# A retention and SoLU kernel: 17 activation tiles transposed by DMA, 16 variances on ScalarE, three more load buffers

## The chip, the cores and the metric

The kernel runs on one core of a Trainium2 chip. The metric is the device time of one execution in microseconds (us), lower is better. A core has TensorE (PE in the profile, with its weight loads as PEld), VectorE (DVE), ScalarE (ACT), GpSimd (POOL), SyncE (SP, which here issues nearly all DMAs) and 16 DMA engines. SBUF is the on-chip memory, PSUM the memory that TensorE writes.

## The reference

Eight batches of eight heads, 576 positions, head size 64; then a feed-forward layer over the 4608 tokens, 512 wide with 1024 inner units.

```python
scores = scale * np.matmul(q, k.transpose(0, 1, 3, 2))
Dmat = np.where(rel >= 0, gamma[:, None, None] ** rel[None, :, :], 0.0)
x = np.matmul(scores * Dmat, v)            # then heads side by side: 4608 x 512
h = x @ w_in
e = np.exp(h - h_max)
solu = h * (e / (np.sum(e, axis=-1, keepdims=True) + 1e-09))
mu, var = mean(solu), mean((solu - mu) ** 2)
out = ((solu - mu) / np.sqrt(var + 1e-06) * g_ln) @ w_out
```

## The kernel before, in words

The sequence of a batch is cut into windows of 256 positions; the last 64 positions of four batches are put together to one more window. That makes 18 windows, and with the two halves of the heads 36 **steps** i. A window has 256 tokens, two **tiles** t of 128 tokens, 36 tiles in all. Tile t belongs to window t//2, so it needs the attention of the steps 2(t//2) and 2(t//2)+1.

Per step: loads of q, k and v by SP (`load`, L373; a step of the joint windows takes four DMAs each) into pool raw, five buffers for each of the three; casts with decay factors on POOL (sq, sk in `scale` L389, cv in `cast_v` L397); transposes T of q and k on PE (`qk_tp` L413), evicted by ACT into pool ev (`tl_ev` L451); scores S on PE (`scores` L499) into the one buffer of PSUM pool s; the mask on DVE (`mask` L536); I, the part that comes from the state (`inter` L475), V, the masked scores times v (`av` L514), and K, the new state (`kv_mm` L524), into pool xy; st, sm, sc on DVE and POOL for the state; xe, the eviction of the attention to xT on ACT (`x_ev` L573).

Per tile: M1 on PE (`mm1` L581, eight matmuls of 512 columns) into the one buffer of pool h; ex on ACT (`exp_` L592); so on DVE (`solu` L597), an f16 tile of 128 x 1024 in pool solu, four buffers; the variance, either bnA and bnB on DVE (`stats` L612) or, for the tiles listed in VA (0 to 3), va on ACT (`squares` L620) with the row sum from so's accumulator and a small fin on DVE (`final` L635); fx on ACT and rs on POOL (`rstd` L644) give the scale of the row, once for a pair of tiles; L, the transposes of solu on PE (`ln_tp` L434), 32 small ones of 64 x 64; Le, its eviction; M2 on PE (`mm2` L653, eight matmuls) with oe on ACT (`o_ev` L664) and the store out (`store` L673), osb having three buffers. M2 writes a buffer of pool s, that of S too; from tile 31 on, odd tiles use pool xy.

From step 10 on, T of step i and L of tile i-6 share one PSUM tile (pool tl, one buffer), and one ACT instruction, TL, evicts both into one buffer of ev. The tiles 30 to 35 have a Le of their own. L of tile t stands ahead of T of step t+6, and M2 of tile t four M1 later than M1 of tile t.

The order on each engine comes from `plan` (L122) and `order_ops` (L233): lists FIRST and LAST fix it by hand for the beginning (on PE to M1 of tile 14) and the end; between them every operation has a due time, and `order_ops` sets the order by the costs of the table DUR. PE's order in the middle is M1, M2, I, L, T, V, K, S (where a tile or step of that kind is there). Six stores (tiles 22 to 27) go as two DMAs of 64 rows (L678). Filling matmuls with zeros (L844) keep PE busy early.

Of the kernel before, what the change touches and what calls it, by code (L numbers as in the profile page):

```python
# [13 lines left out]
P = 128  # L14
# [3 lines left out]
for _b in range(0, B, 4):  # L18
# [5 lines left out]
    T=0.26, L=0.26, Tw=0.45, Lw=0.45, I=0.22, V=0.23, K=0.13, S=0.22, M1=1.73, M2=1.73, M2h=0.87, oeh=0.42, G=0.1, WM=1.73,  # L24
    TL=1.03, Te=0.58, Le=0.58, xe=0.74, ex=1.22, oe=0.69, va=1.25, wiA=0.62, wiB=0.45, wg=0.68, wgD=0.43,
    cvA=0.62, mask=1.22, st=0.58, so=1.22, soA=1.3, bnA=0.68, bnB=0.89, fx=0.2, fin=0.42, wc=0.74, wm=0.62,
    sqD=0.75, gc=0.17, cvD=0.45, sq=1.04, sk=1.04, cv=0.61, sm=0.42, sc=0.81, rs=0.69, rsB=1.0,
    ldx=0.88, ldw=1.36, out=0.65,
)
HOP, PE_OUT = 0.07, 0.2  # L30
# [3 lines left out]
VA = (0, 1, 2, 3)  # L34
ON = {'sq0': 'DVE', 'sq1': 'DVE', 'cv0': 'ACT', 'cv1': 'ACT', 'sk2': 'DVE', 'sk3': 'DVE', 'cv2': 'ACT', 'cv3': 'ACT', 'cv4': 'ACT', 'cv5': 'ACT', 'cv6': 'ACT', 'cv7': 'ACT'}
CAP = dict(
    rawq=5, rawk=5, rawv=5, q16=3, k16=4, v16=4, ev=8, s=1, ret=2, xy=1, gg=6, gt=2, s160=4, s161=9, h=1,
    e=2, solu=4, osb=3, tl=1, tlx=2, tlT=1, tlL=1, wst=5,
# [3 lines left out]
FIRST = dict(  # L42
    PE=(
# [5 lines left out]
    ),  # L49
    ACT=(  # L50
# [4 lines left out]
    ),  # L55
    DVE=(
# [5 lines left out]
    ),  # L62
    POOL=(
# [4 lines left out]
    ),  # L68
    SP=(
# [5 lines left out]
    ),  # L75
)
LAST = dict(
    PE=(
        "I34 L30 V34 S35 M1_32 I35 L31 V35 M2_28 M1_33 M2_29 M2_31 M1_34 L32 M2_30 L33 L34 M1_35 M2_32 M2_33 "
        "L35 cs M2_34 M2_35 M3"  # L80
    ),
    ACT=(
        "oe27 xe34 ex32 Le30 Le31 oe28 xe35 ex33 fx15 oe29 ex34 Le32 oe30 Le33 oe31 fx16 ex35 oe32 Le34 oe33 "
        "Le35 fx17 oe34 oe35 oz"
    ),
    DVE=(
        "so31 mask35 bnA31 so32 bnB31 bnA32 so33 bnB32 so34 bnA34 bnA33 bnB33 bnB34 cnt so35 bnA35 ci bnB35"
    ),
    POOL=(
        "rs15 rs16 rs17"  # L90
    ),
    SP=(
        "out27 out28 out29 out30 out31 out32 out33 out34 out35"
# [11 lines left out]
def ev_T(i):  # L105
    return f"Te{i}" if i < NJ + 2 else f"TL{i - 2}"


def ev_L(t):
    return f"Le{t}" if t < NJ - 4 or t + 4 > NS - 3 else f"TL{t + 4}"  # L110
# [6 lines left out]
def wide(name):  # L117

    return name[0] == "T" and int(name[1:]) < NJ + 2 or name[0] == "L" and int(name[1:]) < NJ - 4


def plan():  # L122
    ops = []
    rank = {n: x - 1e4 for lst in FIRST.values() for x, n in enumerate(lst.split())}
    rank.update({n: x + 1e4 for lst in LAST.values() for x, n in enumerate(lst.split())})
# [6 lines left out]
    for i in range(NS):  # L132
# [20 lines left out]
        jn = i >= NJ + 2  # L153
        op(f"T{i}", "PE", "T" if jn else "Tw", [f"sq{i}", f"sk{i}", f"L{i - 6}" if jn else ""], (n, 0.4), [] if jn else [("tlT", [f"Te{i}"])])
        if jn:
            op(f"TL{n}", "ACT", "TL", [f"T{i}", f"L{i - 6}"], (n, 1.0), [("ev", [f"I{i}", f"S{i}", f"M2_{i - 6}"])])
        else:
            op(f"Te{i}", "ACT", "Te", [f"T{i}"], (n, 1.0), [("ev", [f"I{i}", f"S{i}"])])
        op(f"S{i}", "PE", "S", [ev_T(i)], (i - 1, 0.95), [("s", [f"mask{i}"])])
        op(f"mask{i}", "DVE", "mask", [f"S{i}"], (i - 1, 1.6), [("ret", [f"V{i}"])])  # L160
        kv = i + 2 < NS and i + 2 >= NK and WINS[(i + 2) // 2][1] < 2
        op(f"I{i}", "PE", "I", sdep + [ev_T(i)], (i - 1, 4.75), [("xy", [f"xe{i}", f"st{i + 2}" if kv else ""])])
        op(f"V{i}", "PE", "V", [f"I{i}", f"mask{i}", f"cv{i}"], (i, 0.6))
        op(f"xe{i}", "ACT", "xe", [f"V{i}", f"K{i + 2}" if kv else ""], (i, 2.0))
    for t in range(NT):
# [5 lines left out]
        op(f"so{t}", "DVE", "soA" if va else "so", [f"ex{t}"], (m, 4.56), [("solu", [f"L{t}", f"va{t}" if va else f"bnB{t}"])])  # L171
# [5 lines left out]
        if c:  # L177
# [6 lines left out]
        after = [f"Te{NJ + 1}", f"Le{t - 1}"] if t == NJ - 4 else [f"TL{NS - 3}"] if t + 4 == NS - 2 else []  # L184
        after += [f"Le{t - 2}"] if t - 2 >= NS - 6 else []
        op(f"L{t}", "PE", "Lw" if early else "L", [f"so{t}"] + after, (m + 2, 0.1),
           [("tlL" if early else "tl" if jn else "tlx", [ev_L(t)])])
        if not jn:
# [3 lines left out]
        op(f"M2_{t}", "PE", "M2h" if end else "M2", need, (t + LAG, 3.1), [("h" if end else "xy" if late(t) and t % 2 else "s", [f"oe{t}"])])  # L192
# [40 lines left out]
def order_ops(ops):  # L233
# [24 lines left out]
    while len(start) < len(ops):  # L258
# [14 lines left out]
        if locks(o):  # L273
            lock = end
# [686 lines left out]
```

## Time and profile before

| | |
|---|---|
| three runs | 211.76, 212.97, 213.97 us, median 212.97 |
| span of the profiled execution | 210.9 us; no other time of that execution is recorded |
| granted TensorE clock | 0.999 of full speed |
| share of the span busy | PE 95%, DVE 79%, ACT 67%, POOL 67% |
| moved by DMA | 42.66 MB, 202 GB/s over the span |

How to read the rows that follow: a row of the timeline has start, duration, engine, line, operation, output <- input and the count of merged instructions; in brackets the idle time before it and what ended that. A row of groups has line, engine, operation, shape and count, then busy time and mean ns, then idle time before and its releasers. The ends of matmuls are modelled, so on PE the starts are used here.

### The profile page before, as it was taken

To read this page: it belongs to the slowest core of one execution; us is meant where nothing else is said; L and a number is where in the kernel's file an instruction comes from. 1 tells how busy PE (TensorE), PEld (TensorE's weight loads), DVE (VectorE), ACT (ScalarE), POOL (GpSimd) and SP (SyncE) were. 2 spreads that over 40 slices of the span, in tenths; PEclk is the share of its full clock that TensorE was granted. 3 is DMA by queue.
4 is the path that set the end of the run, shared out by engine and by line. 5 is a ranking of instruction groups with operands and counts; after the bars stand their busy time and mean duration, and the time that the engine had idled before them with its cause. 6 is when DMAs were issued, how large, how long until landed. Compare 5 with 4: busy or idle time off the path is not lost. (4 is left out here: it accounts for less than half of the span.)

```text
span 210.9 us, 10171 instructions
## 1 busy us (share of the span) xinstructions
PE 200.8 (95%) x4400; PEld 113.2 (54%) x4400; DVE 166.1 (79%) x279; ACT 141.7 (67%) x235; POOL 141.7 (67%) x240
## 2 busy tenths in 40 slices
PE   7986989999999999999999999999999999999992
PEld 2442654665566555555555555555666555554451
DVE  6565779997868898978898898889988998753760
ACT  2375787897666776776666777666767777573752
POOL 7434758999997975948787979797979792001110
PEclk9999999999999999999999999999999999999999
DMA  5999999999666559778999686776355222311224
GB/s 157 345 355 334 329 311 269 301 293 306 195 188 188 169 139 278 217 214 259 314 288 305 198 252 183 217 234 181 94 152 153 54 57 67 71 63 54 101 101 104
DMA packets 64814, 42.66 MB, mean 202 GB/s; under 512 B 3320, under 2 KB 58624, under 8 KB 64768
## 3 DMA queue, kind: packets, MB, share of 16 engines
q1 hardware_dynamic: 64528, 41.82, 68.4%
q8 instruction: 34, 0.56, 1.2%
q10 hardware_dynamic: 240, 0.18, 0.5%
q14 instruction: 12, 0.10, 0.2%
HBM read 32.55 MB, written 9.44 MB: 199 GB/s over the span
## 5 line engine op out<-in xcount | busy, mean ns | idle before, releaser
L587 PE MATMUL h_ps<-w_in,xT 128*128 128x512 f16 x288 | 68.5, 380 | 0.0
L660 PE MATMUL o_ps<-w2c,ev 128*128 128x512 f16 (+1 forms) x296 | 67.6, 373 | 0.0
L610 DVE TENSOR_TENSOR solu<-h_ps,e_sb 128x1024 f16<-128x1024 f32 x32 | 39.2, 1223 | 16.7 <-ACT e_sb L595 16.5
L595 ACT ACTIVATE e_sb<-h_ps 128x1024 f32<-128x1024 f32 x36 | 36.8, 1023 | 21.9 <-PE h_ps L587 20.4
L540 DVE TENSOR_TENSOR ret<-s_ps,masks 128x1024 f16<-128x1024 f32 x36 | 43.9, 1220 | 6.0 <-PE s_ps L508 5.4
L660 PEld LDWEIGHTS <-ev 128*128 128x128 f16 x296 | 28.7, 98 | 32.7
L616 DVE BATCH_NORM_STATS2 bs<-solu 128x6 f32<-128x512 f16 x64 | 43.6, 685 | 0.9
L587 PEld LDWEIGHTS <-xT 128*128 128x128 f16 x288 | 25.3, 98 | 29.1 <-ACT xT L576 0.8
L394 POOL TENSOR_TENSOR q<-rawq,small 128x512 f16<-128x512 f32 x34 | 35.4, 1042 | 7.3 <-DMA rawq<-in_q_dram 5.9
L669 ACT ACTIVATE o_sb<-o_ps,rs 128x512 f32<-128x512 f32 (+1 forms) x37 | 25.0, 676 | 21.8 <-PE o_ps L660 10.4
L394 POOL TENSOR_TENSOR k<-rawk,small 128x512 f16<-128x512 f32 x34 | 35.4, 1042 | 6.0 <-DMA rawk<-in_k_dram 5.9
L457 ACT COPY ev<-tl 128x1024 f32<-128x1024 f32 (+1 forms) x32 | 29.7, 932 | 4.7 <-PE tl L429 4.2
L576 ACT CAST xT<-xy 128x512 f16<-128x512 f32 x36 | 26.7, 742 | 3.0 <-PE xy L472 2.9
L571 POOL CAST sbd<-gg 64x256 f16<-64x256 f32 x64 | 25.4, 397 | 3.0
L562 POOL TENSOR_TENSOR gg<-gt,small 128x128 f32<-128x128 f32 x32 | 13.1, 409 | 16.9 <-DVE gt L557 16.5
L648 POOL TENSOR_TENSOR w<-mv,w 128x2 f32<-128x2 f32 x16 | 3.1, 194 | 27.8 <-ACT w L633 13.9
L399 POOL CAST v<-rawv 128x512 f16<-128x512 f32 x28 | 17.1, 609 | 0.2
L508 PE MATMUL s_ps<-ev 64*64 64x128 f16 x576 | 14.8, 218 | 0.3
L472 PE MATMUL xy<-ret,v 64*64 64x128 f16 x576 | 14.7, 217 | 0.0
L472 PEld LDWEIGHTS <-sbd 128*128 128x128 f16 x128 | 9.3, 98 | 9.3 <-issue 1.1
L446 PE MATMUL tl<-ident,solu 64*64 64x64 f16 x1024 | 14.2, 195 | 0.0
L846 PE MATMUL tl<-zeros 128*128 128x512 f16 x41 | 12.7, 445 | 1.3 <-DVE zeros L802 1.3
(71 smaller groups left out, 214.6 us busy)
## 6 DMA issues: line engine op xcount, KB each, us to landing
rawq<-in_q_dram SPq DMA_DIRECT2D x32, 256.0 KB, 5.1
rawk<-in_k_dram SPq DMA_DIRECT2D x32, 256.0 KB, 5.3
rawv<-in_v_dram SPq DMA_DIRECT2D x32, 256.0 KB, 5.1
out_dram<-o_sb SPq DMA_DIRECT2D x26, 256.0 KB, 3.1
out_dram<-o_sb SPq DMA_DIRECT2D x19, 128.0 KB, 2.3
wst<-in_moe_w_in_dram SPq DMA_DIRECT2D x4, 512.0 KB, 6.8
wst<-in_moe_w_out_dram SPq DMA_DIRECT2D x4, 512.0 KB, 7.1
rawq<-in_q_dram SPq DMA_DIRECT2D x16, 64.0 KB, 2.4
```

What stands on the lines that cost most here:

```text
L394: eng.tensor_tensor(out=t.rearrange("p j h d -> p h j d"), in0=st[i]["r" + nm], in1=g, op=ALU.mult)
L457: nc.scalar.copy(out=t[:, lo:hi].rearrange("p x (r w) -> p r x w", r=2), in_=tls[n].rearrange("p r x w -> p (r x w)").bitcast(FP).rearrang ...
L472: nc.tensor.matmul(start=(c, e) not in begun, stop=False, skip_group_check=True, **kw)
L540: nc.vector.tensor_tensor(out=d["ret"].rearrange("p e h j q -> p (e h) (j q)"), in0=d["s"].rearrange("p e h j q -> p (e h) (j q)"), in1=ma ...
L571: nc.gpsimd.tensor_copy(out=t[ee[e], :, :, ee[e]], in_=st[i]["gg"][ee[e]])
L576: nc.scalar.copy(out=xT[:, 2 * w : 2 * w + 2, 2 * hf : 2 * hf + 2].rearrange("p c h (q j) -> p c h j q", j=2), in_=xys[i][:, :, 0:256].rea ...
L587: nc.tensor.matmul(out=h_ps[:, hh], lhsT=xT[:, t, dc], rhs=w_in16[:, dc, hh], start=(dc == 0), stop=(dc == 3),)
L595: nc.scalar.activation(out=d["e"], in_=d["h"], func=ACT.Exp, accum_out=se[:, t : t + 1])
L610: nc.vector.tensor_tensor(out=d["solu"], in0=d["h"], in1=d["e"], op=ALU.mult)
L616: nc.vector.bn_stats(out=d["bs"][:, half], in_=d["solu"][:, half * 512 : half * 512 + 512])
L660: nc.tensor.matmul(out=o, lhsT=d["ev"][:, d["lo"] + c], rhs=w2c16[:, c, mm], start=(c == 0), stop=(c == 7))
L669: nc.scalar.activation(out=d["osb"][:, mm], in_=d["o", half], func=ACT.Copy, scale=ws[t // 2]["rs"][:, t % 2 : t % 2 + 1])
```

## The change

It has five parts.

1. Tiles 18 to 34 (LX): L on PE and its eviction go; SP issues `ln_dma`, one DMA that transposes solu from SBUF to SBUF, into a buffer of ev. The steps 24 to 35 then have a T alone, which ACT evicts with Te, half as wide as TL. L35 remains, with eight transposes of 128 x 128 into a bank of the new pool o2.
2. Tiles 18 to 33 join VA: their variances go from bnA and bnB on DVE to va on ACT, with fin on DVE; rs of these pairs loses one of its two POOL instructions.
3. When the staging buffers of the weights are free, a pool bis with three load buffers each for q, k and v takes their space. `extra` gives it the steps 19 to 21, 27 to 29 and 35.
4. M2 of the tiles 30 to 34 writes pool o2, two buffers in the space of pool tl, in place of s and xy. The stores of the tiles 22 to 27 go whole.
5. The orders of all engines are written out in full (ORDER), with changed costs in DUR behind them; the number of filling matmuls stays. Up to about tile 10 the orders are those of before. In the middle PE's order is M1, M2, I, V, K, T, S, with L gone from tile 18 on. The tail of PE is `S35 M1_32 I35 V35 M2_28 M1_33 M2_29 M2_30 M1_34 M2_31 M2_32 M1_35 M2_33 L35 cs M2_34 M2_35 M3`; before it was `S35 M1_32 I35 L31 V35 M2_28 M1_33 M2_29 M2_31 M1_34 L32 M2_30 L33 L34 M1_35 M2_32 M2_33 L35 cs M2_34 M2_35 M3`.

The options TX, SPL and TWO of the changed code are empty and do nothing. The core of the diff:

```diff
-VA = (0, 1, 2, 3)
+VA = (0, 1, 2, 3, 18, 19, 20, 21, 22, 23, 24, 25, 26, 27, 28, 29, 30, 31, 32, 33)
...
+LX = (18, 19, 20, 21, 22, 23, 24, 25, 26, 27, 28, 29, 30, 31, 32, 33, 34)
+TX = ()
+R0 = 14
+OT = 30
+SPL = ()
+TWO = ()
...
+ORDER = dict(
+    PE=(
...
+        "M2_9 I16 V16 L12 T18 K18 S17 M1_14 M2_10 I17 L13 T19 V17 S18 K19 M1_15 M2_11 I18 V18 L14 T20 K20 S19 M1_16  "
+        "M2_12 I19 L15 T21 V19 K21 S20 M1_17 M2_13 I20 V20 L16 K22 T22 S21 M1_18 M2_14 I21 V21 K23 L17 T23 S22 M1_19  "
+        "M2_15 I22 V22 K24 T24 S23 M1_20 M2_16 I23 T25 V23 K25 S24 M1_21 M2_17 I24 V24 K26 T26 S25 M1_22 M2_18 I25 V25  "
...
+    ACT=(
...
+        "xe24 fx10 va20 ex22 Te26 oe18 va21 xe25 ex23 Te27 oe19 va22 xe26 ex24 Te28 oe20 va23 fx11 xe27 ex25 Te29 oe21  "
...
+    SP=(
...
+        "ldk27 ldv26 ldv27 out12 ldq26 ldq28 ldk29 ldq29 ldk28 ldv28 out14 ldk30 lx18 out13 ldv30 ldv29 ldq30 ldv31  "
+        "ldq31 ldq32 out15 ldk31 out16 ldq33 ldv33 lx19 lx20 ldv32 out17 lx21 ldk32 lx22 out18 lx23 out19 ldk33 ldq34  "
+        "out20 ldk35 out21 ldk34 lx24 lx26 ldv34 lx25 out22 ldq35 lx27 out24 out23 out25 ldv35 lx29 lx28 out26 lx30 lx31  "
+        "out27 lx32 out28 out29 lx33 out30 lx34 out31 out32 out33 out34 out35"
...
 def ev_T(i):
-    return f"Te{i}" if i < NJ + 2 else f"TL{i - 2}"
+    return f"tx{i}" if i in TX else f"Te{i}" if i < NJ + 2 or i - 6 in LX else f"TL{i - 2}"
...
+def extra(i):
+    return i >= R0 and (i - R0) % 8 >= 5
...
+def home(t):
+    return "h" if t == NT - 1 else "o2" if t >= OT else "xy" if late(t) and t % 2 else "s"
...
-    for name in ("q16", "k16", "v16", "ev", "ret", "gg", "gt", "e", "solu", "osb", "wst"):
+    for name in ("q16", "k16", "v16", "ev", "ret", "gg", "gt", "e", "solu", "osb"):
         pool(name, CAP[name])
...
+    loads_w = ExitStack()
+    pools["wst"] = loads_w.enter_context(tc.tile_pool(name="wst", bufs=CAP["wst"]))
...
-        st[i]["r" + nm] = t = pools["raw"].tile([P, 4, 2, D], FP, tag=nm, name="raw" + nm)
+        if extra(i) and "bis" not in pools:
+            loads_w.close()
+            pool("bis", CAP["bisq"])
+        st[i]["r" + nm] = t = pools["bis" if extra(i) else "raw"].tile([P, 4, 2, D], FP, tag=nm, name="raw" + nm)
...
+    def bank():
+        if "o2" not in pools:
+            banks_2.close()
+            pool("o2", CAP["o2"], space=PS)
+        return pools["o2"].tile([P, 512], FP, tag="o2", name="o_ps")
...
+    def blocks():
+        t = pools["ev"].tile([P, 16, 64], FP, tag="ev", name="ev")
+        return t.rearrange("p x w -> p (x w)").bitcast(F16).rearrange("p (x w) -> p x w", w=P)[:, 0:8]
...
+    def ln_dma(t):
+        tk[t]["lo"] = 0
+        tk[t]["ev"] = x = blocks()
+        nc.sync.dma_start_transpose(out=x, in_=tk[t]["solu"])
...
-        nm = "xy" if half or late(t) and t % 2 else "s"
-        nm = "h" if t == NT - 1 and not half else nm
+        nm = "xy" if half else home(t)
         mm = slice(256 * half, 256 * half + (256 if t == NT - 1 else DM))
-        d["o", half] = o = pools[nm].tile([P, 2, 512], FP, tag=nm, name="o_ps")[:, 0, 0 : mm.stop - mm.start]
+        o = bank() if nm == "o2" else pools[nm].tile([P, 2, 512], FP, tag=nm, name="o_ps")[:, 0]
+        d["o", half] = o = o[:, 0 : mm.stop - mm.start]
...
-            n = 64 if 22 <= t < 28 else P
+            n = 64 if t in TWO else P
...
+        elif k_ == "lx":
+            ln_dma(x)
```

More of the change, by code (lines that the diff above doesn't have):

```diff
@@ L33 @@
 NJ, NK, LAG, WE = 8, 8, 6, 0
-VA = (0, 1, 2, 3)
+VA = (0, 1, 2, 3, 18, 19, 20, 21, 22, 23, 24, 25, 26, 27, 28, 29, 30, 31, 32, 33)
 ON = {'sq0': 'DVE', 'sq1': 'DVE', 'cv0': 'ACT', 'cv1': 'ACT', 'sk2': 'DVE', 'sk3': 'DVE', 'cv2': 'ACT', 'cv3': 'ACT', 'cv4': 'ACT', 'cv5': 'ACT', 'cv6': 'ACT', 'cv7': 'ACT'}
 CAP = dict(
-    rawq=5, rawk=5, rawv=5, q16=3, k16=4, v16=4, ev=8, s=1, ret=2, xy=1, gg=6, gt=2, s160=4, s161=9, h=1,
-    e=2, solu=4, osb=3, tl=1, tlx=2, tlT=1, tlL=1, wst=5,
-)
-FIRST = dict(
-    PE=(
[5 rows of a table removed]
+    rawq=5, rawk=5, rawv=5, bisq=3, bisk=3, bisv=3, q16=3, k16=4, v16=4, ev=8, s=1, ret=2, xy=1, gg=6, gt=2, s160=4, s161=9, h=1,
+    e=2, solu=4, osb=3, o2=2, tl=1, tlx=2, tlT=1, tlL=1, wst=5,
+)
+LX = (18, 19, 20, 21, 22, 23, 24, 25, 26, 27, 28, 29, 30, 31, 32, 33, 34)
[4 more added lines that the diff above has]
+TWO = ()
+FILL = {'T0': (0, 3), 'S0': (0, 4), 'K1': (0, 3), 'I0': (0, 2), 'I1': (0, 5), 'M1_0': (0, 5), 'T3': (0, 4), 'I3': (1, 2), 'K6': (0, 1), 'T6': (2, 4)}
+ORDER = dict(
+    PE=(
[11 rows of a table added]
     ),
     ACT=(
[4 rows of a table removed]
[9 rows of a table added]
     ),
     DVE=(
[5 rows of a table removed]
[9 rows of a table added]
     ),
     POOL=(
[4 rows of a table removed]
-    ),
-    SP=(
[5 rows of a table removed]
[L75 to L93, printed above, removed]
[8 rows of a table added]
+    ),
+    SP=(
[9 rows of a table added]
     ),
@@ L183, in plan @@
         early = t < NJ - 4
[L184 to L188, printed above, removed]
+        if t in LX:
+            op(f"lx{t}", "SP", "lx", [f"so{t}"], (m + 2, 0.1), [("ev", [f"M2_{t}"])], DUR["ltx"])
+        lasts = [x for x in range(NT) if NJ - 4 <= x < OT and ev_L(x)[:2] == "Le"]
+        after = [f"Te{NJ + 1}", f"Le{NJ - 5}"] if t == NJ - 4 else []
+        if t in lasts:
+            after += [f"Le{t - 2}" if t - 2 in lasts else ev_T(max(i for i in range(NS) if i not in TX))]
+        if t not in LX:
+            op(f"L{t}", "PE", "Lw" if wide(f"L{t}") else "L", [f"so{t}"] + after, (m + 2, 0.1),
+               [("tlL" if early else "o2" if t >= OT else "tl" if jn else "tlx", [ev_L(t)])])
+        if ev_L(t)[:2] == "Le":
             op(f"Le{t}", "ACT", "Le", [f"L{t}"], (m + 2, 0.95), [("ev", [f"M2_{t}", "M3" if t == NT - 1 else ""])])
@@ L191, in plan @@
         need = [ev_L(t)] + [f"wc{x}" for x in range(8)] + ["cs" if t == NT - 2 else ""]
-        op(f"M2_{t}", "PE", "M2h" if end else "M2", need, (t + LAG, 3.1), [("h" if end else "xy" if late(t) and t % 2 else "s", [f"oe{t}"])])
+        if t == OT:
+            need += [ev_T(max(x for x in range(NS) if x not in TX)), ev_L(max(x for x in range(OT) if x not in LX))]
+        op(f"M2_{t}", "PE", "M2h" if end else "M2", need, (t + LAG, 3.1), [(home(t), [f"oe{t}"])])
         op(f"oe{t}", "ACT", "oeh" if end else "oe", [f"M2_{t}", f"rs{w}"], (t + LAG + 1, 0.1), [("osb", [f"out{t}"])])
@@ L196, in plan @@
             op("oz", "ACT", "oeh", ["M3", f"oe{t}"], (t + LAG + 1, 1.0))
-        op(f"out{t}", "SP", 0.5 if WINS[w][1] < 2 else 0.95, [f"oe{t}", "oz" if end else ""], (t + LAG + 1, 0.85 + end), moved=DUR["out"])
+        op(f"out{t}", "SP", 0.45 if WINS[w][1] < 2 and t not in TWO else 1.2, [f"oe{t}", "oz" if end else ""], (t + LAG + 1, 0.85 + end), moved=DUR["out"])
     for c in range(4):
         op(f"lwi{c}", "SP", 0.47, [], (-4, 0.5 + 0.1 * c), [("wst", [f"wi{c}a", f"wi{c}b"])], DUR["ldw"])
-        op(f"wi{c}a", "ACT", dict(ACT="wiA", DVE="wiB"), [f"lwi{c}"], (1, 0.1 * c))
-        op(f"wi{c}b", "DVE", dict(ACT="wiA", DVE="wiB"), [f"lwi{c}"], (1, 0.1 * c))
+        op(f"wi{c}a", "ACT", dict(ACT="wiA", DVE="wiB", POOL="wiP"), [f"lwi{c}"], (1, 0.1 * c))
+        op(f"wi{c}b", "DVE", dict(ACT="wiA", DVE="wiB", POOL="wiP"), [f"lwi{c}"], (1, 0.1 * c))
     for c in range(0, 8, 2):
@@ L240, in order_ops @@
     pos = {e: 0 for e in todo}
[L241 removed]
+    quad, dma, lock, landed, held, out_at = False, 2.0, 0.0, [], 0.0, 0
     def ready(o):
[L244 removed]
+        t = free[o.eng]
         for d in o.deps:
@@ L766, in emit @@
             tk[x]["lo"] = lo = 8 if wide(f"L{x}") else 8 * (x % 2)
-            tk[x]["ev"] = tl_ev("first" if wide(f"L{x}") else "last", lo, lo + 8)
+            tk[x]["ev"] = tl_ev("first" if wide(f"L{x}") else "last", lo, lo + 8, tk[x].get("tl"))
         elif k_ == "TL":
```

211 lines of the change are left out of this document (135 added, 76 removed), and 61 rows, old and new, of tables (ACT, DVE, PE, POOL).

## The prediction

> **What bounds the kernel now.** I read the page first (busy shares, slices), then the groups by form, then the timeline of single periods, then waits and DMA.
>
> ```profile
> span 210.9 us, 10171 instructions
> PE 200.8 (95%) x4400; PEld 113.2 (54%) x4400; DVE 166.1 (79%) x279; ACT 141.7 (67%) x235; POOL 141.7 (67%) x240
> DMA  5999999999666559778999686776355222311224
> ```
>
> PE is busy nearly all the time, so taking work off PE should pay. But a busy PE only says that the matmuls follow each other; how much of the freed time comes back depends on what else closes within 0.2 us of it. The chain of work on the page is one row long here, so I follow the loop by hand in the timeline (columns: start, duration, engine, line, operation). One period:
>
> ```profile
> 123.62 0.41 PE L508 MATMUL s_ps<-ev 64*64 64x128 f16 x16
> 123.96 1.90 PE L587 MATMUL h_ps<-w_in,xT 128*128 128x512 f16 x8
> 125.70 1.89 PE L660 MATMUL o_ps<-w2c,ev 128*128 128x512 f16 x8
> 125.90 1.02 ACT L595 ACTIVATE e_sb<-h_ps 128x1024 f32<-128x1024 f32 x1 [0.67 <-PE h_ps L587]
> 127.05 1.23 DVE L610 TENSOR_TENSOR solu<-h_ps,e_sb 128x1024 f16<-128x1024 f32 x1 [0.31 <-ACT e_sb L595]
> 127.42 0.28 PE L472 MATMUL xy<-ev,sbd 128*128 128x128 f16 x2
> 127.63 0.45 PE L446 MATMUL tl<-ident,solu 64*64 64x64 f16 x32
> 127.67 0.69 ACT L669 ACTIVATE o_sb<-o_ps,rs 128x512 f32<-128x512 f32 x1 [0.66 <-POOL w L648]
> 127.91 0.30 PE L429 MATMUL tl<-ident,q 64*64 64x64 f16 x16
> 128.51 0.41 PE L508 MATMUL s_ps<-ev 64*64 64x128 f16 x16
> ```
>
> On PE the L transposes occupy the stretch from 127.63 to 127.91, 0.28 us of a period of 4.89. Beside them runs the eviction oe (L669), which ends at 128.36; the next scores S start at 128.51. Both S and M2 write the one buffer of pool s, so S must wait for oe: it has 0.15 us to spare there. The reader is to see that L stands exactly between M2 and S, in the shadow of oe. The next rows show the same loop where L was followed by no T and nothing was left to spare:
>
> ```profile
> 177.81 0.41 PE L508 MATMUL s_ps<-ev 64*64 64x128 f16 x16
> 178.16 1.90 PE L587 MATMUL h_ps<-w_in,xT 128*128 128x512 f16 x8
> 179.89 1.89 PE L660 MATMUL o_ps<-w2c,ev 128*128 128x512 f16 x8
> 181.82 0.69 ACT L669 ACTIVATE o_sb<-o_ps,rs 128x512 f32<-128x512 f32 x1 [0.61 <-PE o_ps L660]
> 182.56 0.42 PE L508 MATMUL s_ps<-ev 64*64 64x128 f16 x16
> ```
>
> S to M1 0.35, M1 to M2 1.73, M2 to oe 1.93, oe 0.69, oe's end to the next S 0.05: 4.75 us. In the first fence M2 to oe is 1.97 (an even tile, whose oe also waits for POOL's rs), which makes 4.79. So the loop S, M1, M2, oe has a floor of 4.77 on average, whatever PE saves between M2 and S.
>
> **The change, part by part.**
>
> *L18 to L34 off PE.* At most 17 x 0.28 = 4.8 us. L18 to L28 stand ahead of the scores of steps 23 to 33 and L29 ahead of step 34, between these rows:
>
> ```profile
> 93.26 0.41 PE L508 MATMUL s_ps<-ev 64*64 64x128 f16 x16
> 118.73 0.41 PE L508 MATMUL s_ps<-ev 64*64 64x128 f16 x16
> ```
>
> From step 22 (118.73) to step 34 (177.81) are 12 periods, 59.08 us, 4.92 each. PE without L could go at 4.64, the loop allows 4.77: 12 x (4.92 - 4.77) = 1.8 us gained. The remaining 0.13 a period becomes a wait of S for oe; late next is oe itself, bound to the end of M2. Step 35 is at the floor already: nothing.
>
> *The DMA transposes on SP.* Seventeen DMAs of 256 KB each are added to SP's queue, and six stores (tiles 22 to 27) that went in halves go whole. The trace has no DMA transpose. Its nearest rows are three issues (bytes, median us to landing); the fourth row is from the waits of SP's own queue (total, times, longest):
>
> ```profile
> out_dram<-o_sb SPq DMA_DIRECT2D x26, 256.0 KB, 3.1
> rawk<-in_k_dram SPq DMA_DIRECT2D x32, 256.0 KB, 5.3
> wst<-in_moe_w_out_dram SPq DMA_DIRECT2D x4, 512.0 KB, 7.1
> SPq L680 <- ACT o_sb L669: 53.8, 24, 5.3
> ```
>
> I take 4 us, between the store of the same size and the load, keep 3.1 and 12 (7.1 with a load of 5.3 ahead of it) as ends. What hides it: M2 of a tile stands four periods behind its M1, and solu is ready 4.4 us after M1 starts (1.94 to ex, 1.15 to so, 1.3 for so with its accumulator), so about 14 us are free in the middle; lx25 and lx28, which the new list puts late, keep 5 or more. Queued behind a waiting lx on SP are stores and loads: lx18 delays out13, lx26 holds ldv34, lx27 holds out24. SP waits 53.8 us for oe in the last row, so it has room, and osb has three buffers, two periods of grace. Cost nothing; without that cover a late store would hold oe and with it S. The DMA line shows 8, 6, 7, 7, 6, 3, 5, 5 tenths in slices 24 to 31 (121 to 163 us), where most transposes fall, so bandwidth is there.
>
> The Trainium skill, "VectorE: DVE Perf Modes", section "The three transpose paths", speaks against the change: one 128 x 128 block costs 390 ns on TensorE and 1309 ns by DMA. The trace does not agree for PE: eight blocks cost 0.28 us here, as 32 small matmuls. By the page a tile would take 8 x 1.309 = 10.5 us (my estimate) if its blocks go one by one. No run so far shows the DMA side; that is the slow rival below.
>
> *ScalarE.* The rows of the groups by form:
>
> ```profile
> L595 ACT ACTIVATE e_sb<-h_ps 128x1024 f32<-128x1024 f32 x36 | 36.8, 1023 | 21.9 <-PE h_ps L587 20.4 <-DVE bs L616 1.4
> L595 ACT ACTIVATION_READ_ACCUMULATOR e_sb<-h_ps 128x1 f32 x36 | 7.0, 194 | 0.0
> L457 ACT COPY ev<-tl 128x1024 f32<-128x1024 f32 x26 | 26.3, 1013 | 4.7 <-PE tl L429 4.2
> L455 ACT COPY ev<-tl 128x512 f32<-128x512 f32 x14 | 8.0, 587 | 4.0 <-PE tl L419 3.4 <-PE tl L439 0.4
> L669 ACT ACTIVATE o_sb<-o_ps,rs 128x512 f32<-128x512 f32 x35 | 24.1, 688 | 21.4 <-PE o_ps L660 10.4 <-POOL w L648 6.0 <-issue 2.0
> L576 ACT CAST xT<-xy 128x512 f16<-128x512 f32 x36 | 26.7, 742 | 3.0 <-PE xy L472 2.9
> L624 ACT ACTIVATE junk<-solu,su 128x1024 bf16<-128x1024 f16 x4 | 4.6, 1148 | 0.0
> L624 ACT ACTIVATION_READ_ACCUMULATOR junk<-solu,su 128x1 f32 x4 | 0.8, 192 | 0.0
> L633 ACT ACTIVATE w<-se 128x2 f32<-128x2 f32 x18 | 3.6, 206 | 0.0
> ```
>
> Added: 16 squares of 1.148 + 0.192, 21.4 us. Removed: 12 joint evictions of 1.013 become evictions of 0.587, and five Le of the last tiles go. A period on ACT is then ex 1.22, Te 0.59, oe 0.69, va 1.34, xe 0.74, half an fx 0.10: 4.68 of 4.77. It fits, by 0.09. Between ex and oe stands Te: ex starts 1.94 after M1 and ends at 3.08, Te at 3.67, oe may start at 1.73 + 1.93 to 1.97 = 3.66 to 3.70: just hidden. va and xe (2.1) follow oe and end at 6.45, the next ex is due at 4.77 + 1.94 = 6.71. Cost nothing, from 0 to 0.1 a period; without cover every 0.1 is 1.2 us.
>
> *VectorE and GpSimd.* DVE loses, for 16 tiles, two bn_stats of 0.685 and an aggregate of 0.209, and gets a read of the accumulator and a small fin per tile:
>
> ```profile
> L616 DVE BATCH_NORM_STATS2 bs<-solu 128x6 f32<-128x512 f16 x64 | 43.6, 685 | 0.9
> L618 DVE BATCH_NORM_AGGREGATE mv<-bs 128x2 f32<-128x12 f32 x32 | 6.7, 209 | 1.1
> L605 DVE SCALAR_TENSOR_TENSOR solu<-h_ps,e_sb 128x1024 f16<-128x1024 f32 x4 | 4.9, 1215 | 0.0
> L605 DVE DVE_READ_ACCUMULATOR solu<-h_ps,e_sb 128x1 f32 x4 | 0.3, 83 | 0.0
> ```
>
> That is 25.3 us off DVE, but so and mask already follow their releasers there: gain nothing. The h loop (M1, ex, so) is 1.94 + 1.15 + 1.30 + 0.05 = 4.44, under 4.77.
>
> *Load buffers and new order, steps 17 to 22.* Steps 17 (93.26) to 22 (118.73) take 25.47 us, 5.09 a period; at 4.92 it would be 24.6. The excess of 0.87 can come back through loads that start earlier (steps 19 to 21 get the new buffers), or not at all, or grow by as much with transfers pulled together. I take 0.3.
>
> *The tail.* Up to the first M1 after step 35 nothing is new. Then:
>
> ```profile
> 197.22 1.90 PE L587 MATMUL h_ps<-w_in,xT 128*128 128x512 f16 x8
> 200.65 1.22 DVE L610 TENSOR_TENSOR solu<-h_ps,e_sb 128x1024 f16<-128x1024 f32 x1
> 206.75 0.47 ACT L669 ACTIVATE o_sb<-o_ps,rs 128x256 f32<-128x256 f32 x1 [0.41 <-PEq L916]
> ```
>
> Before, M1_32 (182.56 + 0.35 = 182.91) to M1_35 takes 14.31. After: 4.44 by the h loop, then twice M1 and two M2 (5.2): 14.84, 0.5 lost. From M1_35 to the last eviction it is 9.53 before. After: so35 ends at 4.31 (here 4.65), then cnt, bn and rs on DVE and POOL (about 3.2) and two evictions (1.1), 8.7: 0.8 gained. Together 0.3 gained, from 0 to 0.6. lx34 has from so34's end (M1_34 + 4.4) to M2_34 (M1_34 + 5.2 + 4.8): 5.6 us, and my 4 fits.
>
> Sum: 1.8 + 0.3 + 0.3 = 2.4 us off the span of 210.9, 208.5. The record gives no other time of the profiled execution; the median of the runs, 212.97, lies 2.07 above this span, so I forecast 210.5.
>
> **The rivals.**
> 1. *All of L's time comes back*, since the loop closes sooner than I think, or steps 17 to 22 give all: 12 x 0.28 = 3.4 + 0.9 + 0.3 = 4.6, 208.4. For it: PE's 95%. Against it: the five rows at 177.81 to 182.56, which have 0.05 to spare.
> 2. *ScalarE becomes the bound.* If the 0.09 is eaten by waits of 0.2 a period (ACT waits for M2 before oe in its rows), a period is 4.88: 0.5 + 0.6 = 1.1 gained, 211.9. For it: a fixed order on an engine 98% full.
> 3. *Slower: the transposes land late.* It decides at lx34: above 5.6 us each us is added, and the 2.4 are gone at 8. At the upper end, 12.2, M2_34 waits 6.6: 212.97 - 2.4 + 6.6 = 217.2. The skill's page named above stands for this side. Against it: the store of the same bytes in 3.1.
>
> **How the numbers follow.** Forecast 0.48, rival 1 0.16, rival 2 0.20, rival 3 0.16. About 1%, 2.1 us, is what a measurement of this kernel tells from no change, so faster is below 210.84. The forecast lies at its edge: 0.42 faster, 0.06 same, for its error reaches further down (0.9 in steps 17 to 22, 0.6 in the tail) than up. Rival 1 is all faster; rival 2 is 0.02 faster, 0.17 same, 0.01 slower; rival 3 is 0.01 same, 0.15 slower. Sum: faster 0.60, same 0.24, slower 0.16. The range leaves out rival 3: below, rival 1 less 0.6; above, no gain at all and 0.6 for the start of rival 3: 207.8 to 213.6.
>
> **What would show it.** Periods of S at 4.73 to 4.80 from step 23, S starting 0.05 after oe's end, and PE idle ahead of S by about 0.13: right. Periods of 4.64 are rival 1. ex starting later than 1.95 after M1's start, with ACT's idle gone, is rival 2. Waits of L660 for a DMA into ev, or a time to landing over 5.6 us, is rival 3. The forecast is wrong in its size if steps 17 to 22 change by more than 0.9 us.

## The result and the profile after

| | before | after |
|---|---|---|
| median of 8 runs each | 212.96 us (211.76 to 214.03) | 211.66 us (210.89 to 212.44) |
| ratio, 95% interval | | 0.9927 (0.9901 to 0.9953) |
| span of the profiled execution | 210.9 us | 209.4 us (its own time 211.14) |

The change gains 0.7%. The prediction said 210.5 us, with 207.8 to 213.6 as its range. In a second set of runs the ratio was 0.9934 (0.9911 to 0.9957). Here and below, medians and ratios leave out slow executions, those over 1.5% above the fastest of their kernel.

The page after, the same three lines as before:

```profile
span 209.4 us, 9045 instructions
PE 197.5 (94%) x3832; PEld 110.1 (53%) x3832; DVE 144.5 (69%) x263; ACT 150.8 (72%) x262; POOL 139.7 (67%) x232
DMA  5999999999766558999999499999649896956544
```

VectorE has lost 21.6 us of work and ScalarE has 9.1 more. PE shows only 3.3 us less with 568 matmuls fewer; as the ends of matmuls are modelled, a short wait can count as busy, so the starts are read. The timeline of one period and the start of the next (columns as before):

```profile
123.53 0.42 PE L619 MATMUL s_ps<-ev 64*64 64x128 f16 x16
123.88 1.90 PE L712 MATMUL h_ps<-w_in,xT 128*128 128x512 f16 x8
125.62 1.89 PE L785 MATMUL o_ps<-w2c,ev 128*128 128x512 f16 x8
125.82 1.02 ACT L720 ACTIVATE e_sb<-h_ps 128x1024 f32<-128x1024 f32 x1
127.34 0.28 PE L579 MATMUL xy<-ev,sbd 128*128 128x128 f16 x2
127.73 0.69 ACT L794 ACTIVATE o_sb<-o_ps,rs 128x512 f32<-128x512 f32 x1 [0.71 <-POOL rs L775]
128.47 0.42 PE L619 MATMUL s_ps<-ev 64*64 64x128 f16 x16
```

S to M1 0.35, M1 to M2 1.74, as before. L is gone from PE, and S starts 0.05 after oe's end (127.73 + 0.69 = 128.42). In this period oe itself is late (2.11 after M2, it waited for POOL's rs), so it is the longest of the steady part, 4.94. The last period before the tail has no such wait, and it is the first in which the profile shows PE idle ahead of S:

```profile
176.35 0.42 PE L619 MATMUL s_ps<-ev 64*64 64x128 f16 x16
176.70 1.90 PE L712 MATMUL h_ps<-w_in,xT 128*128 128x512 f16 x8
178.43 1.89 PE L785 MATMUL o_ps<-w2c,ev 128*128 128x512 f16 x8
180.36 0.69 ACT L794 ACTIVATE o_sb<-o_ps,rs 128x512 f32<-128x512 f32 x1 [0.61 <-PE o_ps L785]
181.10 0.42 PE L619 MATMUL s_ps<-ev 64*64 64x128 f16 x16 [0.20 <-ACT o_sb L794]
```

That is 4.75, the loop of the prediction term by term. Steps 17 and 22, and the tail:

```profile
93.00 0.43 PE L619 MATMUL s_ps<-ev 64*64 64x128 f16 x16
118.78 0.41 PE L619 MATMUL s_ps<-ev 64*64 64x128 f16 x16
196.18 1.89 PE L712 MATMUL h_ps<-w_in,xT 128*128 128x512 f16 x8
204.95 0.47 ACT L794 ACTIVATE o_sb<-o_ps,rs 128x256 f32<-128x256 f32 x1 [0.41 <-PEq L1036]
```

So the 1.5 us of span came from here (before, then after):

| stretch | before | after | gain |
|---|---|---|---|
| up to S17 | 93.26 | 93.00 | 0.26 |
| S17 to S22 | 25.47 | 25.78 | -0.31 |
| S22 to S34 | 59.08 | 57.57 | 1.51 |
| S34 to M1_32 (181.45 after) | 5.10 | 5.10 | 0 |
| M1_32 to M1_35 | 14.31 | 14.73 | -0.42 |
| M1_35 to the start of the last eviction | 9.53 | 8.77 | 0.76 |
| from there to the span's end | 4.15 | 4.45 | -0.30 |

Parts 4 and 5 were not taken out by themselves, so what each of them gives in the tail is not separated. The transposes, from the DMA issues (bytes are those of solu, 256 KB) and from the view of their line (issue on SP min/median/max ns; time to landing):

```profile
ev<-solu SPq DMA_TRANSPOSE x17, 4.3
out_dram<-o_sb SPq DMA_DIRECT2D x32, 256.0 KB, 3.6
```

```profile
L567 SPq DMA_TRANSPOSE ev<-solu x17: 1231/1279/2494, 119.3 to 195.4; - x17
DMA to landing us min/median/max: 3.1/4.3/5.9
```

No M2 waited for one. The longest, 5.9, is over the 5.6 that lx34 may take, but none that long stood in the tail.

### The profile page after: what moved, and what is told of

It is laid out like the page before. It is cut to its first block, busy times and chain, and to the rows that moved or that the text cites. A ratio compares the mean times of both kernels' runs of the same rounds, so it can differ in the third digit from the quotient of the medians.

```text
span 209.4 us, 9045 instructions
## 1 busy us (share of the span) xinstructions
PE 197.5 (94%) x3832; PEld 110.1 (53%) x3832; DVE 144.5 (69%) x263; ACT 150.8 (72%) x262; POOL 139.7 (67%) x232
## 2 busy tenths in 40 slices
DMA packets 82666, 47.06 MB, mean 225 GB/s; under 512 B 21176, under 2 KB 76480, under 8 KB 82624
## 3 DMA queue, kind: packets, MB, share of 16 engines
q1 hardware_dynamic: 82384, 46.28, 85.2%
## 5 line engine op out<-in xcount | busy, mean ns | idle before, releaser
L712 PE MATMUL h_ps<-w_in,xT 128*128 128x512 f16 x288 | 68.4, 380 | 0.1
L730 DVE SCALAR_TENSOR_TENSOR solu<-h_ps,e_sb 128x1024 f16<-128x1024 f32 x20 | 24.5, 1223 | 15.5 <-ACT e_sb L720 15.5
L735 DVE TENSOR_TENSOR solu<-h_ps,e_sb 128x1024 f16<-128x1024 f32 x16 | 19.5, 1222 | 11.5 <-ACT e_sb L720 11.2
L775 POOL TENSOR_TENSOR rs<-w,small 128x2 f32<-128x2 f32 x18 | 12.4, 690 | 18.8 <-DVE w L764 17.8
L549 ACT COPY ev<-tl 128x1024 f32<-128x1024 f32 (+1 forms) x26 | 21.1, 812 | 3.3 <-PE tl L519 3.3
L749 ACT ACTIVATE junk<-solu,su 128x1024 bf16<-128x1024 f16 x20 | 22.8, 1142 | 0.0
L741 DVE BATCH_NORM_STATS2 bs<-solu 128x6 f32<-128x512 f16 x32 | 21.7, 682 | 0.3
```

Of the source, the lines that this page charges most:

```text
L712: nc.tensor.matmul(out=h_ps[:, hh], lhsT=xT[:, t, dc], rhs=w_in16[:, dc, hh], start=(dc == 0), stop=(dc == 3),)
L730: nc.vector.scalar_tensor_tensor(out=d["solu"], in0=d["h"], scalar=1.0, in1=d["e"], op0=ALU.mult, op1=ALU.mult, accum_out=d["su"],)
L741: nc.vector.bn_stats(out=d["bs"][:, half], in_=d["solu"][:, half * 512 : half * 512 + 512])
L749: nc.scalar.activation(out=x, in_=d["solu"], func=ACT.Square, bias=d["su"], scale=-1024.0, accum_out=ws[t // 2]["mv"][:, t % 2, 1:2],)
```

## The experiments

All times are medians, and the ratios are to the kernel before, run beside each kernel on the same chip. As a steady measure that leaves the wait at S24 out, I use the nine periods from S25 to S34:

| kernel | time us | ratio (95%) | S25 to S34, one period |
|---|---|---|---|
| before | 212.96 | 1 | 44.30, 4.92 |
| after | 211.66 | 0.9927 (0.9901 to 0.9953) | 43.13, 4.79 |
| after again | 211.54 | 0.9934 (0.9911 to 0.9957) | 43.18, 4.80 |
| q transposed twice | 213.10 | 1.0007 (0.998 to 1.0035) | 43.76, 4.86 |
| half of S twice | 214.27 | 1.0051 (1.0025 to 1.0078) | 44.09, 4.90 |
| L18 to L29 back on PE | 215.09 | 1.0109 (1.0059 to 1.0158) | 45.29, 5.03 |
| S in two halves | 212.53 | 0.9956 (0.993 to 0.9982) | 43.49, 4.83 |
| variances back on DVE | 211.85 | 0.9958 (0.9921 to 0.9996) | 43.09, 4.79 |
| no extra load buffers | 214.66 | 1.0081 (1.005 to 1.0113) | late transposes, 5.08 |
| DMA from tile 15 | 211.12 | 0.9923 (0.9893 to 0.9953) | 43.08, 4.79 |
| DMA from tile 12 | 216.85 | 1.0166 (1.0107 to 1.0225) | late transposes, 5.02 |
| part 3 alone | 214.86 | 1.0069 (1.0037 to 1.0102) | 44.51, 4.95 |

S25, where the nine periods begin, before and after (S34 stands at 177.81 and 176.35):

```profile
133.51 0.41 PE L508 MATMUL s_ps<-ev 64*64 64x128 f16 x16
```

```profile
133.22 0.43 PE L619 MATMUL s_ps<-ev 64*64 64x128 f16 x16
```

My theory: the loop through the one buffer of pool s (S, M1, M2, oe) sets the period after the change. The rivals: PE's own throughput, ScalarE, VectorE's lighter load, or the transfers.

**Two sides of S.** The same sort of work, put once between M2 and S and once between S and M1. Both kernels repeat matmuls whose results are the same.

```diff
+        qk = [(0, st[i]["q16"]), (1, st[i]["k16"])]
-        for n, src in enumerate((st[i]["q16"], st[i]["k16"])):
+        for n, src in qk[:1] * (24 <= i < 35) + qk:
```

> In steps 24 to 34 the transposes of q in T are made twice (about 0.13 us more of TensorE's work in each of 11 steps, between M2 and the next S). Theory (the loop through the one buffer of pool s sets the period: TensorE waits there for oe's end anyway): hidden, 0 to +0.6 us against the changed kernel's 211.7, S still starting 0.03 to 0.10 us behind oe's end. Rival (TensorE's own throughput sets the period, so any work on it counts): 11 x 0.13 = +1.4 us, 213.1.

```diff
-        for hp in range(2):
+        for hp in (0, 0, 1) if 23 <= i < 35 else (0, 1):
```

> In steps 23 to 34 the first 8 matmuls of S are made twice, so that about as much TensorE work as in the run above (0.13 to 0.20 us a step) lies on the other side, between S's start and M1. Theory (the loop sets the period): each counts in full, 12 x 0.13 to 0.20 = +1.6 to +2.4 us against the changed kernel's 211.7, so 213.3 to 214.1, periods of 4.92 to 4.98 where 4.75 to 4.83 stood. Rival (TensorE's throughput): the same as the run above, whichever side of S the work stands on. Rival (ScalarE's 4.68 us a step sets the period): below +0.8.

The first kernel (q twice: 32 transposes where 16 stood), one step:

```profile
158.33 0.69 ACT L795 ACTIVATE o_sb<-o_ps,rs 128x512 f32<-128x512 f32 x1 [0.19 <-POOL q L477]
158.65 0.42 PE L520 MATMUL tl<-ident,q 64*64 64x64 f16 x32
159.23 0.41 PE L620 MATMUL s_ps<-ev 64*64 64x128 f16 x16
```

The second (S with 24 matmuls where 16 stood), the same step:

```profile
158.99 0.53 PE L619 MATMUL s_ps<-ev 64*64 64x128 f16 x24
159.45 1.90 PE L712 MATMUL h_ps<-w_in,xT 128*128 128x512 f16 x8
```

In the second, S to M1 grows from 0.35 to 0.46, and the period grows by the same 0.11: on the loop everything counts. In the first, S starts 0.21 behind oe's end (159.02), and the period grows by 0.07 of the 0.13 added: half is hidden, half counts. In five of the eleven steps PE reached S 0.19 to 0.26 us after oe had ended. My theory holds for the place and was too generous with the room: about 0.06 us a step of the addition found spare time, not 0.13. In time both kernels lost more than their steps explain: +1.4 and +2.6 against after, of which the nine periods scaled to their 11 and 12 steps give 0.8 and 1.3. Both times are over the theory's, and the first is just the 213.1 of its rival, so the periods have to decide here and not the times. In the two profiles another 0.7 us each went in the steps 17 to 22, which stand before the first added matmul (see the stops below), 0.7 in the first loads of the first kernel, and 1.3 in the end of the last stores of the second. Why the medians moved by more than the added work was not seen.

**The changed kernel a second time.**

> The changed kernel itself a second time, for a second profile. Theory (TensorE's stalls of 0.2 to 1.2 us at fixed places of its instruction stream in steps 17 to 22, and the first steps' 0.7 us, are chance of the transfers): 211.0 to 212.2 us, the stall in front of L15 (0.52 us in the first profile) of another size, S5 anywhere between 38.2 and 39.0 us, and S22 to S34 again 57.4 to 57.8 us. Rival (the stalls belong to the code): the same 0.5 us at the same place.

The profiled execution was the slowest of its set, 213.58 us. Its S22 to S34 is 57.62 (57.57 the first time), so the steady part repeats to 0.05 us. The first loads came 1.3 us later (S5 at 39.58 against 38.26, later than the 39.0 that I had allowed), and PE stopped in the middle of L15, ahead of its last two matmuls. The first profile, then the second:

```profile
107.95 0.22 PE L538 MATMUL tl<-ident,solu 64*64 64x64 f16 x2 [0.52 <-issue]
```

```profile
110.43 0.22 PE L538 MATMUL tl<-ident,solu 64*64 64x64 f16 x2 [1.34 <-issue]
```

"Issue" means that PE waited for nothing that the profile shows. PE stopped at this place in all six profiles of kernels that transpose just the tiles 18 to 34 by DMA and leave the order of S alone (these two, 0.80 and 0.96 in the two kernels above, 0.51 and 0.79 in the next two), and in none of the four with L18 to L29 back on PE, where stops stand at other places. PE's order up to there is the same in all ten, so the order alone does not make the stop.

Where the stops stand tells more. Between 85 and 120 us the fourteen profiles have 21 of 0.15 to 1.34 us. Counted in matmuls, all of them lie whole multiples of 128 apart, to within two; with the weight loads that is 256 instructions of PE. The records of the instruction queue have a transfer of 16 KB for each such place (the last section has the counts). In each of the 21 stops PE went on 1.25 to 1.66 us after the transfer due there had ended: at 107.95 after one that ended at 106.48 here, at 110.43 after 108.78 the second time. In the four kernels without the stop in L15 that transfer ended 1.28 to 1.91 us before PE came, just early enough.

So the theory is half right. Size and first loads are chance and make up most of the 2.4 us between these two executions. The places at which PE can stop are the code's, and PE waits there for its next instructions. Why the transfer for L15 was late in all six, by 0.5 us or more, stays open.

**The parts, one by one.** First the variances alone (VA cut to 0 to 3, bnA and bnB behind so on DVE):

```diff
-VA = (0, 1, 2, 3, 18, 19, ..., 33)
+VA = (0, 1, 2, 3)
```

> The variances of tiles 18 to 33 are VectorE's again (two instructions a tile); transposes by DMA and load buffers stay. Theory (the steady gain is TensorE's and the loop's; ScalarE's squares fit into its idle time): 211.7 +/- 0.4 us, S22 to S34 57.4 to 57.9 us. Rival (ScalarE with 4.68 us a step bounds the changed kernel): faster, -0.5 us or more, periods below 4.75. Rival (the variances off VectorE are what gave the gain, since S's mask was late): +1 us or more.

The nine periods are 4.79, as with the variances on ScalarE. S23 to S24 took 5.34 (4.94 in after), because oe16 waited 1.10 us for rs behind the statistics of tile 17, an effect of my order at that place. Both rivals fall: ScalarE does not bound the changed kernel, and the lighter VectorE brings nothing to the period. The times, 211.85 and 211.54, lie within the theory's 211.7 +/- 0.4, and their intervals overlap.

Then the load buffers (R0 from 14 to 99, so that no step uses pool bis):

> No extra load buffers: all loads go through the five buffers of before; transposes and variances stay as changed. Theory (the three more buffers give loads a head start that the loop doesn't need): S22 to S34 within 0.3 us of 57.6, the time 211.7 +/- 0.6. Rival (the loads that the extra buffers let start early fill the transfer queues at 95 to 115 us and make TensorE's instruction fetches late): -0.5 us, no stall in steps 17 to 22. Rival (without them loads queue behind the transposes and land late): +1 us or more, with waits of the casts for raw tiles in steps 24 to 34.

The last rival is right in its size, 3.1 us against the second set of after, and this part is the dearest. Its way was another: no cast waited for a load in these steps, but transposes stood behind a load. SP's own waits between 110 and 150 us in this kernel, its rows, and the M2 that pays:

```profile
SPq L462 <- POOL q L477: 6.9, 2, 5.7
```

```profile
128.30 7.13 SPq L462 DMA_DIRECT2D rawq<-in_q_dram  x2
140.32 2.87 SPq L567 DMA_TRANSPOSE ev<-solu  x2
144.39 1.90 PE L785 MATMUL o_ps<-w2c,ev 128*128 128x512 f16 x8 [1.60 <-DMA ev<-solu]
```

A load of q waits 5.7 us until POOL has cast an older one out of its buffer, and lx19 and lx20 stand behind it on SP's one queue. They were issued at 131.65 in the changed kernel and at 140.32 here, and S26 and S27 took 5.69 and 6.53. The buffers do not speed the loads; they keep the queue moving that the transposes now share.

Then L18 to L29 back on PE (LX cut to 30 to 34, L ahead of T, Te again TL):

> L18 to L29 are made by TensorE again, together with T24 to T35; only five tiles keep the DMA transpose. Variances and load buffers stay as changed. Theory (the steady gain is L's transposes taken out from between M2 and S): S22 to S34 goes back from 57.6 to about 59.1 us, the time to about 213.2 (the kernel before has 213.0), S starting 0.15 to 0.35 us behind oe's end. Rival (the gain came from DVE's lighter load, the variances, and not from TensorE): the time stays at 211.5 to 212.0.

The gain is lost and more, 5.03 a period. But this edit changes a second thing: ScalarE's 1.00 us eviction of L and T stands where the 0.58 us Te stood, ahead of oe, and oe starts 2.10 after M2 in place of 1.93 to 1.98. So it does not separate the parts. Two runs were meant to mend that:

> As the run with L18 to L29 back on TensorE (variances still on ScalarE), but ScalarE evicts L and T behind oe, as the kernel before does, and not ahead of it. Theory (that run's extra loss came from the 1.00 us eviction ahead of oe): S22 to S34 falls from 60.2 towards 59.1 us, the time to 212.8 to 213.5. Rival (ScalarE has no room for squares and the long evictions together, wherever they stand): stays at 59.9 or more, 214.5 to 215.5.

> L18 to L29 are TensorE's again and the variances of tiles 18 to 33 VectorE's again, ScalarE evicts L and T behind oe as in the kernel before: of the change the three load buffers are left, and the transposes of tiles 30 to 34. Theory (part 3 alone only covers the transfers that part 1 adds, and gives nothing where there are none): S22 to S34 58.9 to 59.3 us as before, the time 212.6 to 213.2. Rival (the buffers have a gain of their own): below 212.3.

225.78 us (ratio 1.0616, 1.057 to 1.0661) and 226.16 us (1.0614, 1.0579 to 1.0649). My edit put the eviction behind the oe of the next step, not of its own, and the next L had to wait for tile tl. PE's waits between 140 and 180 us in the latter kernel:

```profile
PE tl L538 <- ACT ev L549: 8.0, 7, 1.3
```

This says nothing of the parts, only that one buffer of tl makes the eviction's place in ScalarE's list worth 1.3 us a step. The last run has it right:

> L18 to L29 by TensorE and the variances of tiles 18 to 33 by VectorE again, ScalarE evicting each L and T behind the oe of the same step, as the kernel before does (in the two runs before this one the eviction stood one oe later, and TensorE waited 1.3 us a step for tile tl). Of the change the three load buffers are left, and the transposes of tiles 30 to 34. Theory (the gain is part 1's alone; part 3 only covers the transfers that part 1 adds): no wait for tl, S22 to S34 58.9 to 59.3 us as before, S starting 0.12 to 0.36 us behind oe's end, the time 212.5 to 213.4. Rival (the buffers have a gain of their own): below 212.0.

S25 and S34 of this kernel:

```profile
133.96 0.41 PE L619 MATMUL s_ps<-ev 64*64 64x128 f16 x16
178.47 0.41 PE L619 MATMUL s_ps<-ev 64*64 64x128 f16 x16
```

Nine periods of 4.95 and no wait for tl; S starts 0.13 to 0.34 us behind oe's end. That is about the period of before (4.92), and with the variances worth nothing in the period it leaves the steady gain to part 1, in which L off PE and the narrower eviction on ScalarE were not separated. The forecast of the time missed: 214.86 where 212.5 to 213.4 was expected, so without part 1 the rest of the change is slower than the kernel before. Its profiled execution took 213.4, among its fastest, with 0.66 us lost from S22 to S25, mostly to the same wait of oe16 for rs; S22 to S34 is then 59.95, over the 59.3 expected. Where its other executions lost another 1.5 us was not seen.

**Can more be had?** More tiles by DMA (the same edit, from tile 15, around the stores of tiles 12 and 14, and from tile 12):

```diff
-LX = (18, 19, ...
+LX = (15, 16, 17, 18, 19, ...
-    ... out12 ldq26 ldq28 ldk29 ldq29 ldk28 ldv28 out14 ldk30 lx18
+    ... out12 lx15 ldq26 ldq28 ldk29 ldq29 ldk28 ldv28 lx16 lx17 out14 ldk30 lx18
```

> Tiles 15 to 17 are transposed by DMA too, issued behind the stores of tiles 12 and 14. Theory (in steps 20 to 22 S starts 0.34 to 0.77 us behind oe's end because L's 0.28 us stand in front of it on TensorE): up to 0.28 us a step, so -0.4 to -0.9 us against 211.7, S starting 0.05 us behind oe's end in steps 21 and 22. Rival (three more transposes of 4.3 us and 1.3 us of SP each in the fullest stretch of transfers make loads or stores late): 0 to +1.5 us, with stalls in steps 20 to 26.

> Tiles 12 to 14 are transposed by DMA as well as 15 to 34 (23 transposes). Theory (L's 0.28 us stand in front of S in steps 17 to 22 too, S starting 0.14 to 0.37 us behind oe's end there): S16 to S22 falls from 30.4 us without stalls to 29.2, -0.5 to -1.2 us against 211.6. Rival (no room for more transfers at 95 to 115 us, where the engines are busy all the time): 0 to +2 us, with waits of M2 for a transpose or of the casts for a load.

From tile 15, S20 to S22 (in this profiled execution the first loads were 4 us late, so only differences are read):

```profile
112.94 0.42 PE L619 MATMUL s_ps<-ev 64*64 64x128 f16 x16
117.71 0.41 PE L619 MATMUL s_ps<-ev 64*64 64x128 f16 x16
122.51 0.42 PE L619 MATMUL s_ps<-ev 64*64 64x128 f16 x16
```

4.77 and 4.80 where after had 5.04 and 5.16: the theory's 0.28 a step and a little more. The median, 211.12, is where the theory had it, but the ratio, 0.9923 against 0.9927 and 0.9934, does not show a gain; half a microsecond is below what these runs tell apart. From tile 12 the rival holds, and at 216.85 by more than its 2 us. Steps 17 to 20 are quicker (S16 to S20 19.52, after 20.60 with the stop of 0.52 in it), then the waits between 80 and 150 us take back far more. The profiled execution took 218.18 us, where the fastest of the six took 214.74, so these waits need not be as long in the others:

```profile
DVE solu L730 <- DMA ev<-solu: 5.8, 2, 4.2
POOL k L477 <- DMA rawk<-in_k_dram: 4.7, 1, 4.7
PE o_ps L785 <- DMA ev<-solu: 1.9, 1, 1.9
```

So the next so waits for a solu buffer that a late transpose still reads, a cast waits for a load, and M2 waits for a transpose. This is the prediction's third rival, with six more tiles.

And the loop itself: the two banks of S's tile are made two tiles, M2 writes to one alone, the half of S that uses the other goes first, and the mask is two instructions:

```diff
+        order = [(hp, j, c, e) for hp in range(2) for j in range(2) for c in range(2) for e in range(2)]
+        if i >= 9:
+            order.sort(key=lambda x: -x[3])
```

> The two banks of the tile of pool s are two tiles; M2 writes to the first alone, the mask is two instructions of DVE, one for each, and from step 9 on S makes first the half whose bank M2 doesn't use. Eight of S's sixteen matmuls then needn't wait for oe. Theory (the loop M2, oe, S, M1 through the one buffer sets the period): the loop loses what half of S takes, 0.13 to 0.17 us, for some 22 periods: up to -3 us, and -1 to -1.5 us against 211.7 in the twelve steady periods if the first steps have other bounds; the period falls to about 4.62. Rival (ScalarE, 4.68 us a step, becomes the bound): -0.5 us, with ScalarE's chain without gaps. Rival (two masks a step lengthen the way from S to M1): 0 or slower.

Measured: 212.53, 0.9 more than after (the intervals of the ratios touch). The last rival has the result, 0 or slower, but not the way:

```profile
158.07 0.69 ACT L792 ACTIVATE o_sb<-o_ps,rs 128x512 f32<-128x512 f32 x1 [0.19 <-POOL q L477]
158.79 0.57 PE L615 MATMUL s_ps<-ev 64*64 64x128 f16 x16
159.30 1.90 PE L707 MATMUL h_ps<-w_in,xT 128*128 128x512 f16 x8
```

S no longer waits for oe (which ends at 158.76 here; in other steps S starts before it), but S to M1 is 0.51 where 0.35 to 0.38 stood. Here M1 starts 0.54 behind oe's end, and in nine of the twelve steps from S23 to S34 it starts 0.39 to 0.41 behind it, as in after (0.05 and 0.35). So S loses what it gained by starting early and the loop is no shorter. That the order of the halves does it was argued and not tested apart from the second mask. No version that beats the changed kernel beyond doubt was found; an M2 in another PSUM bank of its own was not tried.

## Why the prediction was right, and where its sizes were off

**The loop floor: right.** It was forecast at 4.75 and 4.79; the steady periods after are 4.75 to 4.85, mean 4.79 and 4.80 in two profiles. From step 23 on S starts 0.04 to 0.08 behind oe's end in every step, where before it started 0.12 to 0.31 behind up to S34. Work on the loop counts in full (half of S twice). Rival 1, that all of L's 0.28 comes back, is out.

**Its size: 1.84 forecast, 1.51 and 1.46 measured.** Of the 0.33 missing in the first profile, 0.15 is S24, whose oe waited for rs. The reason was not traced; with the variances back on VectorE that period is longer still, 5.34. The rest is 0.015 a period.

**"PE idle ahead of S by about 0.13": half of it.** PE without L was taken at 4.64 a period, from 4.92 less 0.28. The run with q transposed twice shows about 0.06 to spare, so PE, too, is nearly at the period.

**Steps 17 to 22: wrong in sign.** 0.3 gained was forecast, with 0.87 either way. 0.31 was lost in one profile, within these bounds, and 1.25 in the other (26.72 us), outside them. All six profiles with the stop in L15 took longer here (25.67 to 26.72) than the one before (25.47), and the four with the same order up to S22 and no stop in L15 took 24.96 to 25.59. The step that failed was to take the excess over 4.92 as what earlier loads could return. PE's stop inside L15, 0.5 us or more in every profile of this order, is a wait for instructions and not among the things that loads could return; the kernel before has one of 0.31 at T20.

**ScalarE: cost nothing, right, but its load was overstated.** From step 17 on ex starts 1.93 to 1.94 after M1 in every step but S22 (1.99), and without the 16 squares the period is the same; rival 2 is out. The sum of 4.68 adds rows that overlap by about 0.1 each. Over the nine periods of the changed kernel ScalarE is busy 37.08 us of 43.13, 4.12 of 4.79 a period, so it is 86% full and not 98%. What has no room is the stretch between ex and oe: with the long eviction there oe started 2.10 after M2.

**Load buffers: priced for the wrong thing.** I gave them a possible gain in steps 17 to 22. Their worth is the cover of the transposes on SP; without it 3.1 us are lost. The prediction named the loads and stores queued behind the transposes, and not the transposes queued behind a load that waits for its buffer.

**The transposes: 4 us taken, 4.3 measured** (3.1 to 5.9). The prediction has the upper end once as 12 and once as 12.2, where its own 7.1 and 5.3 make 12.4; nothing hangs on it. Rival 3 did not happen here and does with less cover. The Trainium skill, "VectorE: DVE Perf Modes", section "The three transpose paths", led to an estimate of 10.5 us a tile if blocks go one by one; the trace disagrees, a tile of eight blocks lands in 4.3. The Trainium skill, "Advanced Engine Details and Errata", section "X-Bar Transpose (TRN2)", says that such DMAs are as fast as regular ones. By the landing that is nearly so (3.6 for the store of the same bytes); by the engines' time it is not, as the last section shows.

**The tail: 0.3 forecast, 0.34 measured** up to the last eviction (14.84 and 8.7 forecast, 14.73 and 8.77 measured). Then 0.30 went in the end of the last stores, which the sum left out.

So of the 1.2 us between 210.5 and 211.66 the profile explains 0.9 (0.33, 0.6 in steps 17 to 22, 0.3 at the end, less 0.26 up to S17 and 0.04 in the tail); the rest is within the spread of single executions. The mechanism, the loop, was right; the forecast gain was about twice the measured one, 2.5 us against 1.3. The 211.66 lies above the prediction's own border for faster, 210.84; it had given faster a chance of 0.60 and this outcome 0.24.

## What to carry to other kernels

When an engine looks 95% busy, write down the loop through the scarcest buffer term by term before pricing work taken off that engine: here it closed 0.13 us below the old period, and half of L's time stayed away. Work moved to a DMA queue also has to be priced by what waits ahead of it in that queue's order; three more load buffers, which made nothing faster by themselves, were worth more than twice the whole gain. To see whether a wait has room, add known work on each side of it and compare the periods.

## What the runs showed of the hardware

A DMA transpose of a 128 x 1024 f16 tile costs 1.28 us of issue on SP and lands in 4.3 us, but it is cut small: with 17 of them, packets under 512 B went from 3320 to 21176, 1050 for each tile. The load queue's share of the 16 engines' time rose from 68.4% to 85.2% of the span, some 34 us or 2.0 us a tile, where its 41.82 MB at 68.4% make 0.9 us for 256 KB of ordinary transfers. Both are estimates from these shares; the other profiles with 17 to 23 transposes give 1.6 to 2.2 us a tile. Over the nine periods the engines' busy share went from 0.47 to 0.86. That fits six tiles more being too many; which transfers they pushed back was not traced.

PE stops at a few places of its stream for 0.15 to 1.34 us while the transfers are dense (85 to 120 us). The sizes do not repeat from profile to profile; the places are always some of the same row, 128 matmuls apart. The instruction queue, before and after:

```profile
q8 instruction: 34, 0.56, 1.2%
```

```profile
q8 instruction: 30, 0.49, 1.0%
```

It moved 0.56 MB in 34 transfers before and 0.49 MB in 30 after; PE had 8800 and 7664 instructions (matmuls and weight loads), which makes 64 B each in both and 256 to a transfer, about a period's worth. At each stop the transfer due there was the latest that had ended, and PE went on 1.25 to 1.66 us behind its end. So these stops are waits for late instructions. What makes a transfer late, and why the one for L15 in six kernels and not in the four named, stays open.
